# A mixer and a gated MLP on one core: the MLP's weights in three pieces instead of four, and a new order of loads and steps

## The chip, the core and the metric

The kernel runs on one core of a Trainium2 chip. The metric is the device time of one execution, in microseconds (us); the kernel before has a median of 144.99 us over three runs (144.84 to 145.03). A core has the engines TensorE (PE in the profile; its weight loads are shown apart as PEld), VectorE (DVE), ScalarE (ACT) and GpSimd (POOL), and SyncE (SP), which here only issues transfers. All work at the same time, each through its own instructions in their order.

## What is computed

`x` has 2048 tokens of D = 448 numbers, all tensors in bf16. One branch is a complex diagonal state-space model over the tokens, the other an MLP with F = 1792 hidden columns; the second gates the first.

```python
xn = layernorm(x)
# state-space branch
Lam_bar = exp(dt * Lam);  B_bar = ((Lam_bar - 1) / Lam)[:, None] * B        # Lam, B, C complex, P = 448
h[t] = Lam_bar * h[t-1] + B_bar @ xn[t]
s = 2 * real(C @ h) + xn * Dskip
# MLP branch (it normalises once more)
m = gelu(layernorm(xn) @ w1 + b1) @ w2 + b2                                   # w1 448 x 1792, w2 1792 x 448
out = x + s * silu(m)
```

## The kernel before, in words

**Tiles and stages.** The tokens are worked on in four groups of 512, each of two blocks of 256. Channels lie on the partitions: 448 rows are three tiles of 128 and one of 64, and a matmul takes 64 rows, so that two matmuls work side by side on the two halves of the rows. The hidden layer has 14 column tiles of 128, taken in seven pairs (`NF = 14`). For a group the stages are:

- statistics (L369, L373; `first_stats` L389 for group 0), the factors of the layer norm (`ln_scale`, L431 to L441) and the normalised rows for both branches, `xn` and `xn2` (L410 for the first block, L451 on VectorE and L452 on ScalarE behind it);
- the change of layout: of group 0's first block by TensorE (L415), of all else by a DMA transposition that SP issues (L77), giving `xn2T` for the MLP and `xnT` for the state-space branch;
- mm1 (L667): `xn2T` times w1, in two phases for each pair of column tiles, six matmuls and then eight; behind it gelu with b1 as its bias on ScalarE (L673). Group 0 goes block by block, with 256 columns to a matmul, since its first block is there earlier; the other groups with 512;
- mm2 (L792, L795; L853 for the last group): the hidden layer times w2, then silu on ScalarE (L798);
- bu (L698): `xnT` times the transposed B_bar (`BT`), then a copy (`ue`, `u`), the scan and the combination on VectorE (L747 to L777);
- yt (L816, L817; L866, L869 for the last group): the states times C, then the gate and the sum with x (L824; L871 and L872 for the last group) and the store.

Beside group 0, the kernel computes the constants: Lam_bar and its powers on small tiles (L491 to L584), B_bar (L600 to L602), transposed into `BT` by SP's DMA (L77, `BT<-Bn`), and combinations of C (`CZ`, `CQ`, L601 and L602) from transposed C (`Cr`, `CZ`).

**What sets the order.** Each step is recorded as a task with the names that it reads and writes. `ORDER` (L154) is one written-out list of all task numbers; each engine does its own tasks in that order, and `Plan.emit` (L99) puts a semaphore wait wherever a task needs the result of another engine or of a transfer. `SECOND` (L175) names the tasks that run on the second of two possible engines (`copy`: VectorE or ScalarE; `small`: VectorE or GpSimd). So a task that waits holds up everything behind it on its engine, and a transfer holds up the later transfers of the same issuing engine.

**The weights.** `CH` (L336) cuts the 14 column tiles into pieces of 2, 4, 4 and 4. For each piece `ldw1` (L339) makes one transfer of rows 0 to 383 and one copy that moves rows 320 to 383 to the other half of the partitions (`w1c`). The last 64 rows of w1 come in one transfer for all columns (`w1r`, L348). A column tile of a piece of n tiles is not contiguous: `fcol` (L646) takes every n-th column of the piece. w2 comes in as many transfers (L359). b1's rows are loaded as four rows on four partitions (`brows`) and turned into columns by six small matmuls in `b1_columns` (L556); Dskip's and b2's rows likewise in `skip_columns` (L563, L564).

**SP's order** before, up to the first transposition of B: x of the two first blocks (112, 112 and 224 KB), w1 piece 0 (192), w1r (224), w1 pieces 1 to 3 (384 each), the transposition of xn2 of group 0's second block, x of group 1 (448), w2 (224, 448, 448, 448), the two large pieces of B (336 each), x of group 2 (448), a small piece of B, the transposition of xn2 of group 1, the other small piece of B, x of group 3 (448), then the transpositions: xn of group 0, two of C, three of B, two of C, xn of group 1. ScalarE's queue has the three short rows of the state-space parameters, b1's rows, Dskip's and b2's.

Of the kernel before, what the change touches and what calls it, by code (L numbers as in the profile page):

```python
# [9 lines left out]
BF = dt.bfloat16  # L10
# [138 lines left out]
def dram_ap(t, offset, ap):  # L149
    return bass.AP(tensor=t.tensor, offset=offset, ap=ap)  # L150
# [1 line left out]


ORDER = [int(k) for k in """  # L154
# [19 lines left out]
""".split()]  # L174
SECOND = [int(k) for k in """  # L175
29 31 45 51 53 54 60 61 62 63 64 65 78 79 80 82 83 84 111 181 204 205 206 208 210 212 216 218 220 229 234 236 238 242 250 254 256 258 270 274 278 328
332 338 353 367 368 370 412 427 428 431 446 448 449 462 476 477 491 492 507 514 530 531 532 534 546 552 554 578 581 615 618
""".split()]


# [19 lines left out]
def bass_recurrent_scan__ssm_conv_s5__mixer_channel_mlp__prompt_kernel(  # L200
# [11 lines left out]
    L, D, F = 2048, 448, 1792  # L212
    assert tuple(A_x.shape) == (1, L, D) and tuple(B_w1.shape) == (D, F) and A_Lambda_re.shape[0] == D
    NB, NG, NF, NK = 8, 4, 14, 256
    NW, LEAD = NK + 2, 4
    NS = LEAD + NK + 2

    kb = Plan(nc)
    with ExitStack() as es:
# [3 lines left out]
        ident = SB("ident", [128, 128])  # L223
        mhalf = SB("mhalf", [128, 1, 1], F32)
        dk = SB("dk", [128, 4, NS], F32)
        iota = dk[:, 0, 0:NW]
        sgn = SB("sgn", [128, 4], F32)
        vrows = dk.bitcast(BF)[:, 1, 0:512]
        brows = vrows[32:36, :]
        cw = SB("cw", [128, 32, 4], F32)  # L230
        ang = SB("ang", [128, 5, 2, 2, 4], F32)
        eps = SB("eps", [128, 2], F32)
# [1 line left out]
        w1_sb = SB("w1_sb", [128, 4, F])  # L234
# [8 lines left out]
        drows = vrows[64:66, 64:512]  # L243
# [10 lines left out]
        gT = SB("gT", [128, 2, NF, 512])  # L254
# [25 lines left out]
        psum = es.enter_context(nc.psum_tensor("psum", [128, 8, 512], F32))  # L280
# [11 lines left out]
        def dve(fn, reads=(), writes=()):  # L292
            kb.add("dve", fn, reads, writes)
# [7 lines left out]
        def pe(fn, reads=(), writes=(), split=False):  # L301
            kb.add("pe", fn, reads, writes, split=split)
# [5 lines left out]
        with nc.Block():  # L308
# [9 lines left out]
            pool(lambda e: e.tensor_scalar(sgn[:, 1:2], sgn[:, 0:1], -TWO_PI, None, op0=ALU.mult), ["sgn"], ["sgn1"])  # L318
            pool(lambda e: e.tensor_scalar(sgn[:, 2:3], sgn[:, 0:1], TWO_PI, None, op0=ALU.mult), ["sgn"], ["sgn2"])
            pool(lambda e: e.memset(sgn[:, 3:4], math.pi / 2), ["sgn"], ["sgn3"])  # L320
            dve(lambda e: e.memset(brows[:, 256:512], 0.0), [], ["br"])
            pool(lambda e: e.memset(mhalf[:], -0.5), [], ["mhalf"])
            pool(lambda e: e.memset(eps[:, 0:1], LN_EPS), [], ["eps"])
            pool(lambda e: e.memset(eps[:, 1:2], LN_EPS * LN_EPS), ["eps"], ["eps"])
# [1 line left out]
            def ld(eng, o, i, writes, reads=()):  # L326
                kb.dma(eng, o, i, reads=reads, writes=writes)
# [4 lines left out]
            def ldx(b0, n, reads=()):  # L332
                ld("sp", x_all[:, b0:b0 + n, :, :], dram_ap(A_x, b0 * 256 * D, [[2 * D, 128], [256 * D, n], [D, 2], [1, D]]),
                   [f"x{b}" for b in range(b0, b0 + n)], reads)

            CH = ((0, 2), (2, 4), (6, 4), (10, 4))  # L336
            chunk = [c for c, (_, n) in enumerate(CH) for _ in range(n)]

            def ldw1(c):  # L339
                a, w = CH[c][0] * 128, CH[c][1] * 128  # L340
                ld("sp", w1_sb[:, 0:3, a:a + w], dram_ap(B_w1, a, [[F, 128], [128 * F, 3], [1, w]]), [f"w1_{c}"])
                copy([(w1_sb[0:64, 3, a:a + w], w1_sb[64:128, 2, a:a + w])], [f"w1_{c}"], [f"w1c_{c}"])

            for par in range(2):
                ld("sp", x_all[:, 0, par, :], dram_ap(A_x, par * D, [[2 * D, 128], [1, D]]), [f"x0p{par}"])
            ldx(1, 1)
            ldw1(0)
            ld("sp", w1_sb[64:128, 3, :], dram_ap(B_w1, 384 * F, [[F, 64], [1, F]]), ["w1r"])  # L348
            ld("act", brows[0:3, :], dram_ap(B_b1, 256, [[512, 3], [1, 512]]), ["br0"], ["br"])
            ld("act", brows[3:4, 0:256], dram_ap(B_b1, 0, [[256, 1], [1, 256]]), ["br1"], ["br"])  # L350
            for i, vec in enumerate((A_Dskip, B_b2)):
                ld("act", drows[i:i + 1, :], dram_ap(vec, 0, [[D, 1], [1, D]]), [f"dbr{i}"])
            ldw1(1)
            ldw1(2)
            ldw1(3)
            for ri, bm in enumerate((A_B_re, A_B_im)):
                ld("sp", Bn[:, ri:6:2, 0:D] if ri else Bn[:, 0:5:2, 0:D], dram_ap(bm, 0, [[D, 128], [128 * D, 3], [1, D]]), [f"Bn{ri}"])
                ld("sp", Bn[ri * 64:ri * 64 + 64, 6, 0:D], dram_ap(bm, 384 * D, [[D, 64], [1, D]]), [f"Bn6{ri}"])
            for c, (a, n) in enumerate(CH):  # L359
                ld("sp", w2_sb[:, a:a + n, :], dram_ap(B_w2, a * 128 * D, [[n * D, 128], [D, n], [1, D]]), [f"w2_{c}"])  # L360
# [193 lines left out]
                small(lambda e: e.tensor_tensor(rot[:, 0, 1, 3:4], s512[:, 3:4], sgn[:, 0:1], ALU.mult), ["as", "sgn"], ["rot01b"])  # L554

            def b1_columns():  # L556
                pe([lambda e, k=k: e.matmul(psum[:, 4, 2 + k:11 + k:4], brows[0:4, k:512:4], ident[32:36, 32:35], start=True, stop=True) for k in range(4)]
                   + [lambda e, k=k: e.matmul(psum[:, 4, k:k + 1], brows[0:4, k:256:2], ident[32:36, 35:36], start=True, stop=True) for k in range(2)],
                   ["br", "br0", "br1", "ident"], ["ps4"])
                copy([(b1f[:], psum[:, 4, 0:14])], ["ps4"], ["b1f"])  # L560

# [84 lines left out]
            def fcol(fi):  # L646
                a, n = CH[chunk[fi]]
                return slice(a * 128 + fi - a, (a + n) * 128, n)
# [200 lines left out]
            def mm2_tokens(g, q, bk):  # L849

                gb, P = g % 2, psum[:, bk, 0:D]
                copy([(P, bbc)], ["rows1"], [f"ps{bk}"])
                pe([lambda e, fi=fi: e.matmul(P, gT[:, gb, fi, 128 * q:128 * q + 128], w2_sb[:, fi, :], start=False, stop=fi == NF - 1, skip_group_check=True)  # L853
                    for fi in range(NF)], [f"gT{gb}_{fi}_{h}" for fi in range(NF) for h in range(2)] + [f"w2_{c}" for c in range(4)], [f"ps{bk}"])
                act(lambda e: e.activation(g3[:, q, :], P, ACT.Silu), [f"ps{bk}", f"Ws{g}"], [f"g3_{q}"])

            def yt_tokens(g, q, part, bk):
# [62 lines left out]
            for word in STEPS.split():  # L920
                k, g = word[0], int(word[1])
# [58 lines left out]
```

## Time and profile before

| | |
|---|---|
| median of three runs | 144.99 us (145.03, 144.99, 144.84) |
| the profiled execution | 145.18 us |
| its span, first to last instruction | 143.4 us |
| TensorE's granted clock | 1.00 |
| busy: PE, DVE, ACT, POOL | 137.7, 126.0, 105.9, 24.7 us |
| DMA: moved in all | 16.21 MB, mean 113 GB/s |

All lines of the profile come from one execution, the one of 145.18 us. Times in them count from the start of the span. A row of the timeline gives start, length, engine, line, operation, tiles and the count of instructions that it takes together; in square brackets stands the idle time of the engine before the row and what ended it. Matmuls are pipelined and their ends are modelled, so the distance of two starts says more than a length. A row of transfers gives the size and the time from issue to landing; SPq is SP's time for issuing.

### The profile page before, as it was taken

The numbers are of one execution on the slowest core, as the hardware profiler recorded it, in microseconds if no ns is written. First come the engines' busy times: TensorE is split into PE (matmuls) and PEld (weight loads), VectorE is DVE, ScalarE is ACT, GpSimd is POOL, SyncE is SP. The second block draws the span as 40 slices with busy tenths as digits, with TensorE's granted clock in tenths as the row PEclk, the third lists the DMA queues.
The fourth block names the chain that finished last, engine by engine and source line by source line (L and its number), as shares of the span: only waits on it lengthen the run. The fifth ranks groups of instructions, "written<-read, shape, count | busy, mean of one in ns | idle before, by whom it ended". The sixth has DMA issues, their size and how long they took to land.

```text
span 143.4 us, 3549 instructions
## 1 busy us (share of the span) xinstructions
PE 137.7 (96%) x1422; PEld 90.9 (63%) x1422; DVE 126.0 (88%) x275; ACT 105.9 (74%) x197; POOL 24.7 (17%) x83
## 2 busy tenths in 40 slices
PE   7999998999999989999999999999999999999991
PEld 7879953464455854566558844588777677665560
DVE  2979878998999679999999989993699998999994
ACT  3699959999996879879889359451777999928300
POOL 3389760256000700001000000200000001000000
DMA  4979997799997961010010745099830000003233
GB/s 101 240 238 249 311 331 184 152 245 184 199 189 148 151 134 35 0 32 0 7 32 0 61 108 110 0 199 193 160 126 9 0 5 0 18 5 69 49 119 128
DMA packets 38530, 16.21 MB, mean 113 GB/s; under 512 B 32937, under 2 KB 38066, under 8 KB 38514
## 3 DMA queue, kind: packets, MB, share of 16 engines
q1 hardware_dynamic: 38352, 15.92, 49.5%
q8 instruction: 11, 0.18, 0.5%
q10 hardware_dynamic: 162, 0.07, 0.2%
q14 instruction: 5, 0.04, 0.1%
HBM read 6.09 MB, written 1.84 MB: 55 GB/s over the span
## 4 chain that ended last, share of the span: by engine, by line
PE 63%; DMA 14%; DVE 13%; SPq 4%; ACT 1%; issue 1%; POOL 1%; DVEq 0%; ACTq 0%
PE psum L667 15%; PE psum L698 13%; PE psum L792 9%; PE psum L853 7%; DMA Bn<-in_A_B_re_dram 6%; PE psum L817 5%; DMA xnT<-xn_sb 5%; PE psum L816 5%; PE psum L382 3%; DMA Cr<-in_A_C_im_dram 3%; SPq L78 3%; DVE tmp L601 2%; DVE Bn L602 2%; PE psum L869 2%; PE psum L866 2%; DVE xn_sb L451 2%
## 5 line engine op out<-in xcount | busy, mean ns | idle before, releaser
L667 PE MATMUL psum<-xn2T,w_sb 64*128 64x512 bf16 (+1 forms) x490 | 46.5, 334 | 0.7 <-DMA w_sb<-in_B_w_dram 0.3
L673 ACT ACTIVATE gT<-psum,b1f 128x512 bf16<-128x512 f32 (+1 forms) x70 | 37.5, 607 | 4.5 <-PE psum L667 4.2
L667 PEld LDWEIGHTS psum<-xn2T,w_sb 64*128 64x128 bf16 x490 | 26.6, 108 | 13.9 <-ACT gT L673 1.0
L792 PE MATMUL psum<-gT,w_sb 128*128 128x512 bf16 x126 | 28.0, 379 | 0.7 <-ACT gT L673 0.6
L698 PE MATMUL psum<-xnT,BT 64*128 64x256 bf16 x392 | 25.0, 269 | 0.4 <-DVE u_sb L721 0.4
L698 PEld LDWEIGHTS psum<-xnT,BT 64*128 64x128 bf16 x392 | 19.2, 94 | 6.7 <-issue 1.0
L792 PEld LDWEIGHTS psum<-gT,w_sb 128*128 128x128 bf16 x126 | 11.9, 98 | 15.6 <-issue 1.5
L757 DVE TENSOR_TENSOR_SCAN s_w<-vs,dk 128x1048 f32<-128x1048 bf16 (+1 forms) x8 | 16.3, 2057 | 0.1
L452 ACT ACTIVATE xn_sb<-x_all,lnw 128x448 bf16<-128x448 bf16 (+2 forms) x16 | 10.0, 665 | 5.4 <-DMA xnT<-xn_sb 3.8
L853 PE MATMUL psum<-w_sb,gT 128*128 128x448 bf16 x56 | 10.9, 352 | 0.0
L474 ACT ACT_TABLE_LOAD x8 | 10.3, 1283 | 0.4
L305 ACT ACTIVATE ue<-psum 128x512 bf16<-128x512 f32 (+1 forms) x12 | 6.4, 562 | 5.3 <-PE psum L698 5.2
L451 DVE TENSOR_SCALAR xn_sb<-x_all,lnw 128x448 bf16<-128x448 bf16 (+2 forms) x24 | 8.0, 362 | 0.9 <-DVE lnw L441 0.5
L853 PEld LDWEIGHTS psum<-w_sb,gT 128*128 128x128 bf16 x56 | 5.5, 98 | 4.8 <-ACT psum L305 0.2
L305 ACT ACTIVATE vs<-s_w 64x258 bf16<-64x258 f32 (+2 forms) x11 | 6.5, 612 | 2.7 <-DVE s_w L757 2.6
L816 PE MATMUL psum<-hx,CZ 128*128 128x256 bf16 x63 | 8.4, 275 | 0.0
L817 PE MATMUL psum<-Bn,CQ 128*128 128x256 bf16 x63 | 8.2, 273 | 0.2 <-DVE Bn L777 0.2
L767 POOL TENSOR_TENSOR cur<-ang 128x8 f32<-128x8 f32 x2 | 0.4, 204 | 41.6 <-DVE ang L766 41.6
L798 ACT ACTIVATE g_sb<-psum,db 128x512 bf16<-128x512 f32 (+1 forms) x12 | 7.1, 629 | 0.6 <-PE psum L792 0.6
L369 DVE BATCH_NORM_STATS2 lnst<-x_all 128x6 f32<-128x448 bf16 x12 | 7.1, 613 | 0.4 <-DMA x_all<-in_A_x_dram 0.4
L816 PEld LDWEIGHTS psum<-hx,CZ 128*128 128x128 bf16 x63 | 5.9, 98 | 2.3 <-issue 0.4
L824 DVE TENSOR_TENSOR t<-psum,g_sb 128x512 bf16<-128x512 f32 (+1 forms) x12 | 7.1, 614 | 0.1
(161 smaller groups left out, 207.1 us busy)
## 6 DMA issues: line engine op xcount, KB each, us to landing
x_all<-in_A_x_dram SPq DMA_DIRECT2D x3, 448.0 KB, 4.3
w_sb<-in_B_w_dram SPq DMA_DIRECT2D x3, 448.0 KB, 5.3
out_dram<-Bn SPq DMA_DIRECT2D x6, 224.0 KB, 2.7
w_sb<-in_B_w_dram SPq DMA_DIRECT2D x3, 384.0 KB, 5.5
w_sb<-in_B_w_dram SPq DMA_DIRECT2D x2, 224.0 KB, 4.5
Bn<-in_A_B_im_dram SPq DMA_DIRECT2D x1, 336.0 KB, 6.5
Bn<-in_A_B_re_dram SPq DMA_DIRECT2D x1, 336.0 KB, 8.5
out_dram<-w_sb SPq DMA_DIRECT2D x3, 112.0 KB, 1.8
```

The costliest lines, as they stand in the source:

```text
L305: kb.either(("act", [lambda e, o=o, i=i: e.activation(o, i, ACT.Copy) for o, i in pairs]), ("dve", [lambda e, o=o, i=i: e.tensor_copy(o, i ...
L451: kb.either(("dve", [lambda e, o=o, i=i: e.tensor_scalar(o, i, rs, nb, op0=ALU.mult, op1=ALU.add) for o, i in parts]), ("act", [lambda e, ...
L452: ("act", [lambda e, o=o, i=i: e.activation(o, i, ACT.Identity, bias=nb, scale=rs) for o, i in parts]),
L474: kb.add("act", lambda e: e.preload_act_table_set(what), reads, writes, sem=name)
L667: return lambda e: e.matmul(dst(bk[k]), w1_sb[rows, d, fcol(2 * j + k)], rhs[rows, d], start=not second and n == 0, stop=second and n == 3)
L673: act(lambda e, k=k, fi=fi: e.activation(gT[:, gb, fi, cols], psum[:, bk[k], cols], ACT.Gelu_apprx_tanh, bias=b1f[:, fi:fi + 1]), ["b1f", ...
L698: fns.append(lambda e, rows=rows, bank=bank, m=m, o=o, n=n: e.matmul(psum[:, bank, c * NK:(c + 1) * NK].rearrange("p (b c) -> p b c", b=2) ...
L757: dve(lambda e, so=so, vi=vi, di=di: e.tensor_tensor_scan(so, vi, di, 0.0, ALU.add, ALU.mult), ["v", "vl", "vz", "dk", "dk01"] + ["v3"] * ...
L792: pe([lambda e, fi=fi: e.matmul(psum[:, bk, :], w2_sb[:, fi, 128 * j:128 * j + 128], gT[:, gb, fi, :], start=fi == 0, stop=fi == NF - 1) f ...
L816: pe([lambda e, k=k: e.matmul(par(psum[:, bk, :], 1), CZ[:, k, cols], halves(hx[:, hb, k, 1:NK + 1]), start=False, stop=k == 6, skip_group ...
L817: pe([lambda e, k=k: e.matmul(par(psum[:, bk, :], 0), CQ[:, k, cols], halves(hz[:, hb, k, :]), start=False, stop=k == 6, skip_group_check= ...
L853: pe([lambda e, fi=fi: e.matmul(P, gT[:, gb, fi, 128 * q:128 * q + 128], w2_sb[:, fi, :], start=False, stop=fi == NF - 1, skip_group_check ...
```

## The change

- `CH` has three pieces, of 4, 4 and 6 column tiles: w1 and w2 come in three transfers each (w1: 384, 384 and 576 KB; w2: 448, 448 and 672 KB) and there are three `w1c` copies. The stride in `fcol` is 4, 4 and 6 instead of 2, 4, 4 and 4.
- `w1r` is issued by ScalarE's queue, behind the three parameter rows and recorded ahead of w1's first piece.
- b1's rows are loaded by SP in two transfers (two rows of 512, one of 768) behind w1's first piece, at another place in the same scratch tile; `b1_columns` has ten small matmuls instead of six. Dskip's and b2's rows are loaded by SP behind w1's last piece.
- The new `ORDER` and `SECOND` have three tasks less (one transfer of w1, one `w1c` copy, one transfer of w2).

SP's order becomes: x of the two first blocks, w1 piece 0, b1's two transfers, w1 pieces 1 and 2, Dskip's and b2's rows, x of group 1, the transposition of xn2 of group 0's second block, the two large pieces of B, w2 (three transfers), x of group 2, a small piece of B, x of group 3, the other small piece of B, then the transpositions: xn2 of group 1, one of C, one of B, one of C, one of B, xn of group 0, the last of B, two of C, xn of group 1.

TensorE's order: mm1 of group 0 takes the pieces in nearly the same way; behind mm2 of group 0, the first bu phase of group 0 stands after 84 of the 98 mm1 matmuls of group 1 instead of after all 98, and further bu phases stand ahead of and among mm2 of group 1. At the very end, on VectorE, one product and sum of an earlier tile of tokens (L871, L872) stands behind the combination of the first half of the last scan instead of ahead of it.

Engines: on VectorE instead of GpSimd, ten small operations of a sine's polynomial (L502 to L506); on VectorE instead of ScalarE, two `w1c` copies and the copy of b1's columns; on GpSimd instead of VectorE, `ln_scale` of group 1 (five operations there, ten on VectorE), three operations that reduce an angle (L499 to L501, in the order ahead of L396 and L397 of group 0's second block) and three other small ones.

The diff, with `ORDER` and `SECOND` cut out:

```diff
@@ -152,29 +152,28 @@
 ORDER = [int(k) for k in """
...
@@ -226,7 +225,7 @@
-        brows = vrows[32:36, :]
+        brows = dk.bitcast(BF).rearrange("p i c -> p (i c)")[32:35, 2 * NS:2 * NS + 768]
@@ -318,7 +317,7 @@
-            dve(lambda e: e.memset(brows[:, 256:512], 0.0), [], ["br"])
+            dve(lambda e: e.memset(brows[:, 512:768], 0.0), [], ["br"])
@@ -333,7 +332,7 @@
-            CH = ((0, 2), (2, 4), (6, 4), (10, 4))
+            CH = ((0, 4), (4, 4), (8, 6))
@@ -344,15 +343,14 @@
             ldx(1, 1)
+            ld("act", w1_sb[64:128, 3, :], dram_ap(B_w1, 384 * F, [[F, 64], [1, F]]), ["w1r"])
             ldw1(0)
-            ld("sp", w1_sb[64:128, 3, :], dram_ap(B_w1, 384 * F, [[F, 64], [1, F]]), ["w1r"])
-            ld("act", brows[0:3, :], dram_ap(B_b1, 256, [[512, 3], [1, 512]]), ["br0"], ["br"])
-            ld("act", brows[3:4, 0:256], dram_ap(B_b1, 0, [[256, 1], [1, 256]]), ["br1"], ["br"])
-            for i, vec in enumerate((A_Dskip, B_b2)):
-                ld("act", drows[i:i + 1, :], dram_ap(vec, 0, [[D, 1], [1, D]]), [f"dbr{i}"])
+            ld("sp", brows[0:2, 0:512], dram_ap(B_b1, 0, [[512, 2], [1, 512]]), ["br0"], ["br"])
+            ld("sp", brows[2:3, :], dram_ap(B_b1, 1024, [[768, 1], [1, 768]]), ["br1"], ["br"])
             ldw1(1)
             ldw1(2)
-            ldw1(3)
+            for i, vec in enumerate((A_Dskip, B_b2)):
+                ld("sp", drows[i:i + 1, :], dram_ap(vec, 0, [[D, 1], [1, D]]), [f"dbr{i}"])
@@ -554,8 +552,8 @@
             def b1_columns():
-                pe([lambda e, k=k: e.matmul(psum[:, 4, 2 + k:11 + k:4], brows[0:4, k:512:4], ident[32:36, 32:35], start=True, stop=True) for k in range(4)]
-                   + [lambda e, k=k: e.matmul(psum[:, 4, k:k + 1], brows[0:4, k:256:2], ident[32:36, 35:36], start=True, stop=True) for k in range(2)],
+                pe([lambda e, k=k: e.matmul(psum[:, 4, k:5 + k:4], brows[:, k:512:4], ident[32:35, 32:34], start=True, stop=True) for k in range(4)]
+                   + [lambda e, k=k: e.matmul(psum[:, 4, 8 + k:9 + k], brows[:, k:768:6], ident[32:35, 34:35], start=True, stop=True) for k in range(6)],
@@ -851,7 +849,7 @@
-                    for fi in range(NF)], ... + [f"w2_{c}" for c in range(4)], [f"ps{bk}"])
+                    for fi in range(NF)], ... + [f"w2_{c}" for c in range(len(CH))], [f"ps{bk}"])
```

More of the change, by code (lines that the diff above doesn't have):

```diff
@@ L154 @@
 ORDER = [int(k) for k in """
[19 rows of a table removed]
[18 rows of a table added]
 """.split()]
 SECOND = [int(k) for k in """
-29 31 45 51 53 54 60 61 62 63 64 65 78 79 80 82 83 84 111 181 204 205 206 208 210 212 216 218 220 229 234 236 238 242 250 254 256 258 270 274 278 328
-332 338 353 367 368 370 412 427 428 431 446 448 449 462 476 477 491 492 507 514 530 531 532 534 546 552 554 578 581 615 618
+21 25 27 42 43 44 53 54 57 60 71 74 75 76 77 80 83 84 85 108 110 173 174 177 182 201 202 203 205 207 209 211 213 215 217 226 229 231 233 235 237 241
+245 249 253 270 326 331 339 360 364 399 400 429 443 446 451 459 471 472 473 487 489 515 529 542 551 561 575 578 612 615 616
 """.split()]
@@ L853, in mm2_tokens @@
                 pe([lambda e, fi=fi: e.matmul(P, gT[:, gb, fi, 128 * q:128 * q + 128], w2_sb[:, fi, :], start=False, stop=fi == NF - 1, skip_group_check=True)
-                    for fi in range(NF)], [f"gT{gb}_{fi}_{h}" for fi in range(NF) for h in range(2)] + [f"w2_{c}" for c in range(4)], [f"ps{bk}"])
+                    for fi in range(NF)], [f"gT{gb}_{fi}_{h}" for fi in range(NF) for h in range(2)] + [f"w2_{c}" for c in range(len(CH))], [f"ps{bk}"])
                 act(lambda e: e.activation(g3[:, q, :], P, ACT.Silu), [f"ps{bk}", f"Ws{g}"], [f"g3_{q}"])
```

37 rows, old and new, of the table ORDER are left out of this document.

## The prediction

> **What bounds the kernel now.** The page comes first, then the busy time by stages, then the order of TensorE's own work.
>
> ```profile
> span 143.4 us, 3549 instructions
> PE 137.7 (96%) x1422; PEld 90.9 (63%) x1422; DVE 126.0 (88%) x275; ACT 105.9 (74%) x197; POOL 24.7 (17%) x83
> ```
>
> TensorE is busy for 96% of the span, VectorE (DVE) for 88%, so the first question is where TensorE itself stands still. The windows below are the stages; their columns are the length, then PE, PEld, DVE, ACT and POOL busy, TensorE's granted clock, the DMA share and GB/s.
>
> ```profile
> 0.00:7.40 7.40, 6.23 (x68) 5.74 (x70) 4.29 (x15) 3.95 (x11) 2.98 (x20) 1.00 0.71 176
> 7.40:13.10 5.70, 5.56 (x96) 4.80 (x98) 4.88 (x22) 5.47 (x14) 4.95 (x12) 1.00 0.82 210
> 13.10:18.70 5.60, 5.60 (x105) 5.37 (x100) 5.07 (x20) 5.50 (x15) 4.53 (x19) 1.00 0.95 329
> 18.70:30.50 11.80, 11.21 (x77) 5.63 (x75) 10.41 (x41) 9.94 (x18) 3.72 (x18) 1.00 0.88 225
> 30.50:41.50 11.00, 10.80 (x102) 5.20 (x99) 10.50 (x25) 10.56 (x17) 3.35 (x5) 1.00 1.07 188
> 41.50:52.80 11.30, 10.81 (x145) 7.31 (x142) 9.68 (x24) 8.41 (x15) 2.92 (x5) 1.00 0.83 147
> 52.80:118.70 65.90, 65.73 (x702) 43.34 (x701) 59.73 (x98) 49.79 (x92) 2.00 (x6) 1.00 0.31 62
> ```
>
> From 52.8 us on TensorE is full (65.73 of 65.90), at clock 1.00: no edit there can win anything while the matmuls are the same, and the change leaves their number alone but for four tiny ones. What can be won lies ahead of 52.8 us: the first 7.4 us, in which the real matmuls have not begun, and 0.59 + 0.20 + 0.49 = 1.28 us of idle time in the three windows from 18.7 to 52.8. Where those are, TensorE's timeline shows (start, length, work, count, idle before and releaser):
>
> ```profile
> 21.80 0.81 PE L792 MATMUL psum<-gT,w_sb 128*128 128x512 bf16 x3
> 23.20 5.77 PE L792 MATMUL psum<-gT,w_sb 128*128 128x512 bf16 x26 [0.59 <-ACT gT L673]
> ...
> 30.55 3.84 PE L667 MATMUL psum<-xn2T,w_sb 64*128 64x512 bf16 x34
> 34.60 7.14 PE L667 MATMUL psum<-xn2T,w_sb 64*128 64x512 bf16 x64 [0.20 <-ACT gT L673]
> 41.57 0.82 PE L698 MATMUL psum<-xnT,BT 64*128 64x256 bf16 x12
> 42.52 3.19 PE L792 MATMUL psum<-gT,w_sb 128*128 128x512 bf16 x14
> 45.65 2.58 PE L698 MATMUL psum<-xnT,BT 64*128 64x256 bf16 x44
> ...
> 49.81 0.83 PE L698 MATMUL psum<-xnT,BT 64*128 64x256 bf16 x12
> 51.00 1.26 PE L698 MATMUL psum<-xnT,BT 64*128 64x256 bf16 x20 [0.36 <-DVE u_sb L721]
> ```
>
> A matmul's end is modelled late, so I count from start to start, with a steady pitch from an undisturbed row. mm2: 5.77/26 = 0.22, so three end at 21.80 + 0.66 = 22.46 and the hole to 23.20 is 0.74. mm1 of 512 columns: (41.57 - 34.60)/64 = 0.109, so 34 end at 34.25 and the hole to 34.60 is 0.35. bu: 2.58/44 = 0.059, so 12 take 0.70; the holes at 42.52 and 51.00 are 0.25 and 0.49. Together 1.83 us: what the changed order could win here at most.
>
> **The change part by part.** First the start, up to the first real matmul (L667).
>
> ```profile
> 2.18 2.73 SPq L78 DMA_DIRECT2D w_sb<-in_B_w_dram  x5
> w_sb<-in_B_w_dram SPq DMA_DIRECT2D x1, 224.0 KB, 4.6
> 6.11 0.57 ACT L305 ACTIVATE xn2T<-psum 128x512 bf16<-128x512 bf16 x1
> 6.11 0.30 PE L557 MATMUL psum<-ident,dk 4*128 4x3 bf16 x4
> 7.36 11.41 PE L667 MATMUL psum<-xn2T,w_sb 64*128 64x256 bf16 x196 [0.34 <-DMA w_sb<-in_B_w_dram]
> ```
>
> SP issues five w1 transfers in 2.73 us, 0.55 each; the 224 KB of w1's last rows are the second, so they start at about 2.7 and land 4.6 later, at 7.3. That is what the first L667 matmul waits for; its other operand is ready at 6.11 + 0.57 = 6.68. With these rows on ScalarE's queue, ahead of the first w1 piece, they no longer stand last. In their place the first piece grows from 192 to 384 KB and two loads of b1's rows follow it on SP. Lower bound: the first matmul at 6.68, a gain of 0.68. Upper bound: x (448 KB), the rows (224) and the piece (384) make 1056 KB where 864 had to land; the 192 KB more take 0.58 at the 329 GB/s of the window from 13.1. In addition there are ten little b1 matmuls instead of six, which were hidden behind the wait; four more at 0.30/4 are 0.30 if nothing hides them, so +0.88. By 7.40 the chip had moved 176 x 7.4 = 1302 KB, more than the 1056 KB, so the new order of bytes need not be late. I take +0.1, between ends of -0.68 and +0.88.
>
> The w1 pieces 2 and 3 now have one transfer and one 64-row copy (L305/L306) less behind them. The copies go from ScalarE to DVE; DVE is idle for 5.70 - 4.88 = 0.8 us and 5.60 - 5.07 = 0.5 us in the two windows from 7.4 to 18.7, which covers them. Dskip's and b2's rows move from ScalarE's queue to SP behind w1: 0.55 each of SP's time; behind them stands x of group 1, which gains more than that (below). Zero.
>
> ```profile
> 9.48 1.33 SPq L77 DMA_TRANSPOSE xn2T<-xn_sb  x1
> xn2T<-xn_sb SPq DMA_TRANSPOSE x1, 3.2
> 9.70 0.19 POOL L431 TENSOR_SCALAR lnw<-lnmv 128x4 f32<-128x4 f32 x1
> 12.95 0.48 POOL L435 TENSOR_SCALAR lnw<-lnw 128x8 f32<-128x8 f32 x1
> ```
>
> The second block of group 0 lands at 9.48 + 3.2 = 12.68 and TensorE comes to it at 7.36 + 98 x 11.41/196 = 13.07: 0.4 of slack. In the new order GpSimd does three more little operations of about 0.2 ahead of that block's square root, so the transposition lands about 0.6 later, and TensorE waits **+0.2** (0 to +0.5).
>
> Now x of group 1 and B ahead of w2.
>
> ```profile
> 15.21 1.68 DVE L369 BATCH_NORM_STATS2 lnst<-x_all 128x6 f32<-128x448 bf16 x3 [0.39 <-DMA x_all<-in_A_x_dram]
> 21.24 1.09 ACT L452 ACTIVATE xn_sb<-x_all,lnw 128x384 bf16<-128x384 bf16 x2 [1.52 <-DVE xn_sb L451]
> ```
>
> The hole of 0.74 at 22.46 is a queue on ScalarE: the two gelus that mm2 needs stand behind group 1's normalisation, which takes ScalarE from 21.24 to 22.33 and waited 1.52 for its turn because x of group 1 landed only at 15.2. In the new order x stands right behind w1: with the first 448 KB of x and w1's 1568, its own 448 end 2464 KB, of which 1302 have moved by 7.4; the other 1162 at 210 to 329 GB/s make 10.9 to 12.9, say 12. This hole goes. What takes its place could be w2: x (896 KB, two groups), w1 with its rows (1568), B (672) and w2 (1568) are 4704 KB. The windows moved 1302 + 1197 + 1842 = 4341 KB by 18.7, then 225 KB per us; with some 230 KB of transposition w2's end is at 18.7 + 593/225 = 21.3. Its last piece is wanted about where the hole stands now, at 22.5, so 1.2 us to spare; if it came later than that, mm2 would wait for the difference. On the other side, group 1's scale (L431 to L435) moves from DVE to GpSimd, where group 0's took 9.70 to 13.43 = 3.7 us. If all of that came on top, the 3.2 that x gains would cover most of it, and DVE's own steps for it are gone. The holes of 0.35 at 34.60 (gelu's table late), 0.25 and 0.49 go because group 1's work is done earlier and the bu phases are spread among mm1: **-1.83** for all four (-0.74 if it is the first alone).
>
> The price of the new order is on SP's queue of transpositions:
>
> ```profile
> 22.45 2.91 SPq L77 DMA_TRANSPOSE xn2T<-xn_sb  x1
> ...
> 26.72 3.25 SPq L77 DMA_TRANSPOSE xnT<-xn_sb  x1
> ...
> 33.70 9.83 SPq L77 DMA_TRANSPOSE BT<-Bn  x3
> BT<-Bn SPq DMA_TRANSPOSE x3, 5.0
> ```
>
> Now group 0's xnT goes out at 26.72, right behind group 1's xn2T. In the new order two transpositions of C and two of B go between them. The two of C took the time from 26.72 + 3.25 = 29.97 to 33.70, 3.73 together; one of B takes 9.83/3 = 3.28. If xn2T goes out at 22.0, a little before the 22.45 of now, xnT is issued at 22.0 + 2.91 + 3.73 + 6.56 = 35.2 at the latest and lands 5.0 later (the row of B's; its own kind follows it in the queue as those do), at 40.2; I take 39.9, as B's first one then finds its operand long ready. TensorE wants xnT earlier than before: the first bu phase now stands after 84 of the 98 mm1 matmuls. With mm1 of group 1 begun at about 30.0 (30.55 - 0.74 + 0.2), that is 30.0 + 84 x 0.109 = 39.1. So TensorE waits **+0.8**; ends 0 and +2.4 (xn2T at 23.3). DVE's writes of group 1's xn buffer wait for the same transposition, and have the mm2 of group 1 as cover.
>
> ```profile
> 139.81 1.06 DVE L871 TENSOR_TENSOR w_sb<-psum,w_sb 128x448 bf16<-128x448 f32 x2 [0.16 <-PE psum L866]
> ```
>
> At the end, DVE takes one product and sum of an earlier token tile after the last scan's half instead of before it. One L871 is 0.53 and DVE has only 0.16 idle there: **+0.3** (0 to +0.5).
>
> Sum: +0.1 + 0.2 - 1.83 + 0.8 + 0.3 = **-0.43**. The span becomes 143.4 - 0.4 = 143.0; the profiled execution, 145.18, is 1.78 more than its span, so 144.75 there. The median of the runs, 144.99, is 0.19 under the profiled execution: 144.56, say 144.5.
>
> **The rivals.** *xnT too late* (slower). SP's queue is serial and DMA's share is already 1.07 from 30.5 to 41.5. The gain is used up when xnT lands at 39.9 + 0.5 = 40.4 rather than 39.9; at 41.5, which an xn2T sent out at 23.3 gives (36.5 + 5.0), the wait is 2.4 instead of 0.8: 144.5 + 1.6 = 146.1; the middle of this case, between 145.3 and 146.1 and with a tail above, is 145.9. For it: DVE is busy 10.41 of 11.80 from 18.7 on, and B's scaling, which two of the transpositions need, is its work. Against it: x and B are there about 3 us earlier, so that scaling can begin earlier.
>
> *The start pays for the bytes.* If all 16 DMA engines are shared, the rows on ScalarE's queue bring nothing and the first matmul pays +0.88 instead of +0.1: 145.3, no measurable change or barely slower. For it: shares of 0.71 and 0.82 around 7.4 us. Against: the 1302 KB. [...]
>
> *Weights at a stride of six.* A piece of six tiles holds a tile's columns six elements apart. The nearest rows are the weight loads at a stride of two and of four:
>
> ```profile
> L667 PEld LDWEIGHTS psum<-xn2T,w_sb 64*128 64x128 bf16 x10 | 0.6, 97 | 0.0
> L667 PEld LDWEIGHTS psum<-xn2T,w_sb 64*128 64x128 bf16 x6 | 0.3, 110 | 0.0
> ```
>
> 97 ns and 110 ns; carried on, some 125 ns at six. The two row halves of a pair run side by side, each with its own load. With 256 columns a matmul takes 0.053 us (5.60/105, the gapless window) to 0.058 (11.41/196), so a pair takes 107 to 116 ns and the 42 pairs of six tiles in two blocks could each lose 9 to 18 ns: 0.4 to 0.75 us; nothing with 512 columns, where a pair takes 218 ns. That makes up to 145.2: no change. Against: 110 is over 107 already, and the window has no idle time. [...]
>
> *Hidden anyway.* The holes are only moved: mm2 waits for w2 or the table instead of the gelus. Then -0.74 or so is not won: 145.2.
>
> **How the numbers follow.** The forecast 0.5, with its own range 143.8 to 145.0. xnT too late 0.22. The start 0.12. Stride six 0.08. Hidden anyway 0.08. About 0.2%, 0.29 us, is what a measurement of this kernel tells from no change: 144.70 to 145.28. The forecast gives 0.44 faster and 0.06 same; the three small rivals together (0.28) 0.08 faster, 0.15 same, 0.05 slower; xnT 0.02 same, 0.20 slower: 0.52, 0.23, 0.25. The range, 143.3 to 146.0: below, xnT just in time (-0.8) and the start at a gain; above, the middle of the xnT case.
>
> **What would show it.** Right: the first L667 matmul at 7.1 to 7.8, the second block at 13.2 to 13.5, no mm2 wait for a gelu at 22 us, mm1 of group 1 at 29.7 to 30.2, one wait of 0.3 to 1.5 for xnT at 39 us and no other hole over 0.3 until 52. Wrong: a first matmul at 8 or later; a pair pitch over 120 ns in tiles 8 to 13; a wait for w_sb in mm2; a bu that starts after 41; or new idle time of TensorE behind 52 us, which I count at nothing.

## The result, and the profile after

The changed kernel takes 145.99 us (median of five runs, 145.68 to 146.59) against 144.84 for the kernel before in the same session: 0.84% slower, ratio 1.0084 with a 95% interval of 1.0057 to 1.011. A second session gave 1.0105 (1.0054 to 1.0156). The forecast was 144.5, faster. All lines of the profile after come from one execution, of 146.59 us.

```profile
span 144.9 us, 3550 instructions
PE 136.8 (94%) x1422; PEld 92.1 (64%) x1426; DVE 126.3 (87%) x280; ACT 102.8 (71%) x190; POOL 26.9 (19%) x79
```

The span is some 1.4 us longer (144.86 against 143.45 before rounding). Where, three coarse windows of each kernel tell (columns as in the prediction); first before, then after.

```profile
5.00:55.00 50.00, 48.25 (x548) 31.09 (x546) 44.28 (x136) 43.85 (x85) 21.04 (x63) 1.00 0.91 206
55.00:97.00 42.00, 41.83 (x395) 26.49 (x395) 40.38 (x68) 31.44 (x56) 1.58 (x4) 1.00 0.26 48
97.00:140.00 43.00, 43.00 (x445) 29.15 (x442) 37.91 (x63) 28.40 (x52) 0.67 (x3) 1.00 0.26 62
```

```profile
5.00:55.00 50.00, 47.28 (x568) 33.02 (x569) 45.54 (x143) 40.49 (x76) 21.78 (x57) 1.00 0.87 206
55.00:97.00 42.00, 41.84 (x372) 26.21 (x373) 38.81 (x66) 33.57 (x59) 2.08 (x5) 1.00 0.32 55
97.00:140.00 43.00, 43.00 (x447) 28.58 (x442) 38.53 (x63) 26.64 (x50) 1.35 (x3) 1.00 0.18 47
```

TensorE's idle time from 5 to 55 us was to fall; by these windows it rose from 1.75 to 2.72 us. About 0.5 of that rise is not real: for 126 weight loads of mm2 the trace has only 122 matmuls, and three of the four missing records each leave a stretch of 0.16 us marked "issue" before 55 us.

```profile
L790 PE MATMUL psum<-gT,w_sb 128*128 128x512 bf16 x122 | 27.0, 379 | 0.6 <-issue 0.6
L790 PEld LDWEIGHTS psum<-gT,w_sb 128*128 128x128 bf16 x126 | 12.0, 98 | 14.5 <-issue 0.4
```

So the idle time is some 2.2 us, still not less than before. From 55 to 140 the two are alike, and TensorE's last matmuls end at 140.44 and 140.54. So the 1.4 us lie behind TensorE's end. TensorE's timeline of the changed kernel shows what became of the holes:

```profile
7.50 6.05 PE L665 MATMUL psum<-xn2T,w_sb 64*128 64x256 bf16 x98
14.85 5.54 PE L665 MATMUL psum<-xn2T,w_sb 64*128 64x256 bf16 x98 [1.30 <-ACT gT L671]
...
20.82 9.01 PE L790 MATMUL psum<-gT,w_sb 128*128 128x512 bf16 x41 [0.16 <-issue]
29.77 1.72 PE L793 MATMUL psum<-gT,w_sb 128*64 128x256 bf16 x28
31.42 9.30 PE L665 MATMUL psum<-xn2T,w_sb 64*128 64x512 bf16 x84
40.94 0.83 PE L696 MATMUL psum<-xnT,BT 64*128 64x256 bf16 x12 [0.23 <-DMA xnT<-xn_sb]
```

mm2 of group 0 (20.82) runs without a hole where 0.74 us stood, and mm1 of group 1 (31.42) without the one of 0.35. But the second block begins only at 14.85, 1.3 us after the first block's end. The releaser named there, a gelu, is not it: the block's transposition, issued at 9.78, landed 4.9 us later, at 14.7.

```profile
xn2T<-xn_sb SPq DMA_TRANSPOSE x1, 4.9
```

The end, on SP's queue (start, length of issuing), before and after:

```profile
135.35 2.17 SPq L78 DMA_DIRECT2D out_dram<-Bn  x2
139.74 1.79 SPq L78 DMA_DIRECT2D out_dram<-w_sb  x4
```

```profile
138.80 0.81 SPq L78 DMA_DIRECT2D out_dram<-Bn  x2
141.48 1.79 SPq L78 DMA_DIRECT2D out_dram<-w_sb  x4
```

VectorE's steps that count here, before and after (the sums into `Bn` are group 2's, those into `w_sb` the last group's):

```profile
133.61 0.22 DVE L841 TENSOR_TENSOR Bn<-Cr,x_all 128x128 bf16<-128x128 bf16 x1
134.78 0.55 DVE L838 TENSOR_TENSOR Bn<-Cr,x_all 128x768 bf16<-128x768 bf16 x1
...
139.08 0.56 DVE L872 TENSOR_TENSOR w_sb<-w_sb,x_all 128x448 bf16<-128x448 bf16 x2
...
140.79 0.57 DVE L872 TENSOR_TENSOR w_sb<-w_sb,x_all 128x448 bf16<-128x448 bf16 x2
```

```profile
137.25 0.55 DVE L836 TENSOR_TENSOR Bn<-Cr,x_all 128x768 bf16<-128x768 bf16 x1
137.72 0.38 DVE L870 TENSOR_TENSOR w_sb<-w_sb,x_all 128x448 bf16<-128x448 bf16 x1
...
138.56 0.21 DVE L839 TENSOR_TENSOR Bn<-Cr,x_all 128x128 bf16<-128x128 bf16 x1
...
140.89 0.45 DVE L870 TENSOR_TENSOR w_sb<-w_sb,x_all 128x224 bf16<-128x224 bf16 x2
```

VectorE ends at 141.34, where it ended at 141.36 before. Yet the first of SP's four last stores, whose data was there at 137.72 + 0.38 = 138.10, goes out at 141.48, 3.4 us later, and from there all four follow in a row. From VectorE's end to the end of the span it is 3.5 us; before, 2.1. SP is done with issuing group 2's stores at 139.61 and then stands for 1.9 us, and no engine's work ends that wait.

It stands in the function that writes out the program, `Plan.emit`: at the fourth of SP's tasks from the end, SP waits for all transfers recorded so far.

```python
settle = [t for t in order if t.eng == "sp"][-4]
...
if t is settle:
    for sem, val in self.counts.items():
        if val and sem not in ENGS and seen.get(sem, 0) < val:
            eng.wait_ge(self.sems[sem], val)
```

In both kernels those transfers include group 2's two stores (`out_dram<-Bn`). The new order computes two of their sums (L836, L839; L838 and L841 before) between the last group's, so the stores go out at 138.80 to 139.6 instead of 135.35 to 137.5, and take 2.1 us to land. Only then may the last group's stores start.

The section on the change says that a product and a sum of L871 and L872 moved behind the first half of the last scan's combination. That is wrong: in `ORDER` these steps stand behind both halves in either kernel. What moved are the two sums of group 2, from ahead of that combination to behind the first product of the last group, and with them group 2's two stores.

### The profile page after: what moved, and what is told of

It is laid out like the page before. It is cut to its first block, busy times and chain, and to the rows that moved or that the text cites. A ratio compares the mean times of both kernels' runs of the same rounds, so it can differ in the third digit from the quotient of the medians.

```text
span 144.9 us, 3550 instructions
## 1 busy us (share of the span) xinstructions
PE 136.8 (94%) x1422; PEld 92.1 (64%) x1426; DVE 126.3 (87%) x280; ACT 102.8 (71%) x190; POOL 26.9 (19%) x79
## 4 chain that ended last, share of the span: by engine, by line
PE 67%; DVE 6%; DMA 3%; ACT 2%; issue 1%; SPq 0%; DVEq 0%
PE psum L665 16%; PE psum L696 15%; PE psum L790 12%; PE psum L851 7%; PE psum L814 5%; PE psum L815 5%; DMA xnT<-xn_sb 3%; DVE Bn L600 2%; PE psum L793 2%; PE psum L864 2%; PE psum L819 2%; ACT WT L582 2%; DVE tmp L599 2%; DVE w_sb L869 1%; PE psum L867 1%
## 5 line engine op out<-in xcount | busy, mean ns | idle before, releaser
L665 PEld LDWEIGHTS psum<-xn2T,w_sb 64*128 64x128 bf16 x490 | 27.4, 116 | 14.0 <-ACT gT L671 2.2
L790 PE MATMUL psum<-gT,w_sb 128*128 128x512 bf16 x122 | 27.0, 379 | 0.6 <-issue 0.6
L765 POOL TENSOR_TENSOR cur<-ang 128x8 f32<-128x8 f32 x3 | 2.3, 757 | 55.3 <-DVE ang L764 55.3
L472 ACT ACT_TABLE_LOAD x8 | 10.3, 1283 | 0.4
L449 DVE TENSOR_SCALAR xn_sb<-x_all,lnw 128x448 bf16<-128x448 bf16 (+2 forms) x29 | 9.5, 358 | 0.3 <-DMA xnT<-xn_sb 0.2
L304 ACT ACTIVATE vs<-s_w 64x258 bf16<-64x258 f32 (+2 forms) x14 | 7.9, 571 | 2.4 <-DVE s_w L755 2.3
L814 PE MATMUL psum<-hx,CZ 128*128 128x256 bf16 x63 | 7.9, 275 | 0.0
L431 POOL TENSOR_TENSOR lnw<-lnw,mhalf 128x8 f32<-128x8 f32 x4 | 7.2, 1812 | 0.3
```

Of the source, the lines that this page charges most:

```text
L304: kb.either(("act", [lambda e, o=o, i=i: e.activation(o, i, ACT.Copy) for o, i in pairs]), ("dve", [lambda e, o=o, i=i: e.tensor_copy(o, i ...
L449: kb.either(("dve", [lambda e, o=o, i=i: e.tensor_scalar(o, i, rs, nb, op0=ALU.mult, op1=ALU.add) for o, i in parts]), ("act", [lambda e, ...
L472: kb.add("act", lambda e: e.preload_act_table_set(what), reads, writes, sem=name)
L665: return lambda e: e.matmul(dst(bk[k]), w1_sb[rows, d, fcol(2 * j + k)], rhs[rows, d], start=not second and n == 0, stop=second and n == 3)
L790: pe([lambda e, fi=fi: e.matmul(psum[:, bk, :], w2_sb[:, fi, 128 * j:128 * j + 128], gT[:, gb, fi, :], start=fi == 0, stop=fi == NF - 1) f ...
L814: pe([lambda e, k=k: e.matmul(par(psum[:, bk, :], 1), CZ[:, k, cols], halves(hx[:, hb, k, 1:NK + 1]), start=False, stop=k == 6, skip_group ...
```

## The experiments

The theory of the end: SP's collective wait, now behind later stores, costs 1.4 us. Its rival: VectorE's order alone, as the prediction had it. In the edits `move(a, b)` puts task a ahead of task b in `ORDER`; what stands behind a # is added here.

**e1_tail**, the end put back:

```diff
+move(638, 654)  # q01
+move(636, 655)  # o01
+move(640, 662)  # store of block 1
+move(639, 671)  # store of block 0
```

> The changed kernel with group 2's last two sums on VectorE and the two stores of group 2 put back to where they stood before (ahead of the last scan's combination). Theory: the 1.4 us lost behind TensorE's end is SP waiting, ahead of its four last stores, for group 2's stores to land; so the span falls by 1.3 to 1.5 us against the changed kernel and the last four stores go out from about 139.8 instead of 141.5. Rival: only VectorE's own order costs, the 0.3 us of the prediction; then it falls by 0.3 or less, and the stores still go out at about 141.

Measured: 145.12 us, ratio to before 1.001 (0.9984 to 1.0035); span 143.6.

```profile
135.89 1.34 SPq L78 DMA_DIRECT2D out_dram<-Bn  x2
138.94 3.06 SPq L78 DMA_DIRECT2D out_dram<-w_sb  x4
```

**e2_settle**, no task moved:

```diff
-        settle = [t for t in order if t.eng == "sp"][-4]
+        settle = [t for t in order if t.eng == "sp"][-6]
```

> The changed kernel with nothing moved, but SP's collective wait for all earlier transfers put ahead of its sixth store from the end instead of the fourth, so that it no longer covers group 2's stores. Theory of SP's wait: the span falls by 1.2 to 1.4 us although VectorE's order is the changed one. Rival (VectorE's order, or the last stores colliding on the DMA engines): no change, within 0.3 us.

Measured: 145.12 us, ratio 1.0015 (0.9991 to 1.0039); span 143.8.

```profile
139.10 0.81 SPq L78 DMA_DIRECT2D out_dram<-Bn  x2
139.96 2.19 SPq L78 DMA_DIRECT2D out_dram<-w_sb  x4
```

Group 2's stores are as late as in the changed kernel, but the last ones no longer wait for them. The span fell by 1.1 us with VectorE's order untouched, which the rival excludes. The stretch from VectorE's end to the end of the span says it without what happens earlier in an execution: it is 2.24 us in e1, e2 and all the later kernels that are built on e1, 2.1 in the kernel before, p1 and p2, and 3.5 to 3.8 in the four profiles of kernels whose wait covers late stores (after, after_again, e3, e4).

**e3_before_late**, the kernel before with the late sums and stores:

```diff
+move(639, 685)  # o01
+move(641, 685)  # q01
+move(643, 694)
+move(642, 694)
```

> The kernel before with only this done: group 2's last two sums on VectorE and its stores behind the product of the first token tile, as in the changed kernel. Theory of SP's wait: 1.0 to 1.5 us slower than before. Rival (VectorE's order alone): 0.3 us slower or less.

Measured: 146.83 us, ratio 1.0132 (1.0087 to 1.0176): 1.9 us slower, more than expected. From VectorE's end to the end of the span it is 3.8 us, 1.7 more than before; that is SP's wait. But VectorE itself also ends later here, at 142.20 instead of 141.36: the two moved sums (0.55 and 0.22) stand among the last group's. So the edit costs by both theories, and it is e2, not this run, that separates them. Without the wait (e1, e2) the change is level with before: everything else of it nets to nothing.

Why nothing? First suspect: the second block's late transposition.

**e4_w2_first**: `move(34, 32)`, w2's first piece behind it instead of B's.

> The changed kernel with the first piece of w2 (rows of 3584 B) instead of the first piece of B (rows of 896 B) right behind the transposition of group 0's second block on SP's queue. Theory a: the small packets of B hold up the last completions of the transposition; then its landing goes from 4.9 to about 3.3 us, the hole of 1.3 us at 14.85 closes and the span falls by up to 1.3 us. Rival b: an instruction fetch of 16 KB, which runs for 0.94 us on one of the DMA engines just when the transposition ends, holds them up, and the follower doesn't matter; then the hole stays at 1 us or more.

Measured: 147.08 us, ratio 1.0135 (1.0098 to 1.0173). The transposition landed after 3.8 us and the hole before the second block shrank to 0.18, but the first bu phase then waited 2.05 us for xnT and began at 41.67. Closing the hole won nothing, since the next bound lies behind it; the run without an edit says the same. Whether the order of the loads made the landing late, this run can't tell, because the late landing also goes away without an edit.

**after_again**, nothing edited.

> The changed kernel once more, nothing edited. If the late landing of the second block's transposition comes from an instruction fetch that falls at another time in each execution, then the fetch ahead of 14 us and the hole before the second block differ from the first profile (12.68 us, 1.3 us); if it comes from the order of the loads, both are the same again.

Measured: 146.30 us, ratio 1.0105; the fetch at 10.15 us, landing after 3.1 us, no hole before the second block, mm1 of group 1 at 30.52 instead of 31.42, and yet:

```profile
30.52 9.29 PE L665 MATMUL psum<-xn2T,w_sb 64*128 64x512 bf16 x84
40.85 0.83 PE L696 MATMUL psum<-xnT,BT 64*128 64x256 bf16 x12 [1.03 <-DMA xnT<-xn_sb]
```

The first bu phase begins at 40.85, as at 40.94 in the first profile. xnT's landing sets it.

**before_again**, nothing edited.

> The kernel before once more, nothing edited. Same question: with the fetch as the cause, its time differs from the 12.07 us of the first profile, and if it falls between 10.5 and 12 us the second block's transposition lands late here too; with the order of loads as the cause it lands at about 12.7 us again.

Measured: one run, 144.19 us; the second block's transposition landed after 3.2 us, as in the first profile of that kernel, so this run doesn't tell the two causes apart. Its profile shows something else too: of the four holes that the prediction counted, those of 0.35 (in mm1 of group 1) and of 0.49 (between the bu phases) are not there, with nothing edited.

```profile
30.64 10.89 PE L667 MATMUL psum<-xn2T,w_sb 64*128 64x512 bf16 x98
...
49.60 2.49 PE L698 MATMUL psum<-xnT,BT 64*128 64x256 bf16 x42
```

**e5_xnt_early**: e1_tail with `move(184, 219)`, xnT ahead of B's transpositions.

> The changed kernel with its end put right as in e1_tail, and group 0's transposition xnT ahead of the first transposition of B on SP's queue, so that only one of C stands ahead of it. Theory: after mm1 the next bound is xnT's landing (40.9 to 41.7 us in the runs so far); it should now land by 36, the wait for it (0.2 to 2.0 us) goes, and the first bu phase begins at 39.7, or at 40.7 if the second block is late; the time falls by 0.5 to 1.0 us against e1_tail, to 144.1 to 144.6. Rival: the transpositions of B, each now 1.1 us later, become the bound instead, and nothing is won (145.1).

Measured: 145.91 us, ratio 1.0082 (1.005 to 1.0113). The rival held in its mechanism: the same phase begins at 40.82 and waits for B instead. But the time is 0.8 us above the rival's 145.1; a second wait of 0.6 us, for ScalarE, is new, and the rest was not traced.

```profile
PE psum L706 <- DMA BT<-Bn: 1.4, 1, 1.4
PE psum L706 <- ACT tmp L608: 0.6, 1, 0.6
```

**e6_xn_before_wt**: e1_tail with `move(182, 197)`, the one ScalarE step for which VectorE stood still.

> The changed kernel with its end put right as in e1_tail, and one ScalarE step moved: the last normalisation of group 0 (27.1 us in the changed profile), for which VectorE stands still for 1.03 us, ahead of the four conversions of the state tables at 24.71. Theory: the first bu phase waits for a chain that runs through VectorE's scaling of B and SP's serial transpositions, and this is its one slack; so that phase begins at 39.8 to 40.2 instead of 40.8 to 41.3 and the time falls by 0.5 to 1.0 us against e1_tail. Rival: SP's queue alone, from the moment when xn2T goes out (24.0), sets it; then the first bu phase stays at 40.8 or later and nothing is won.

Measured: 145.03 us, ratio 1.0008 (0.9976 to 1.0039). The rival held: the phase begins at 40.80. SP's queue shows why; each transposition occupies SP for 1.5 to 3.1 us, and each row starts where the one before ends:

```profile
24.26 2.16 SPq L77 DMA_TRANSPOSE xn2T<-xn_sb  x1
26.47 1.55 SPq L77 DMA_TRANSPOSE Cr<-in_A_C_re_dram  x1
28.07 3.14 SPq L77 DMA_TRANSPOSE BT<-Bn  x1
31.24 1.97 SPq L77 DMA_TRANSPOSE Cr<-in_A_C_im_dram  x1
33.26 2.85 SPq L77 DMA_TRANSPOSE BT<-Bn  x1
36.15 1.92 SPq L77 DMA_TRANSPOSE xnT<-xn_sb  x1
```

**e8_xn2_early**: e6 with `move(268, 206)`, `move(269, 206)`, `move(270, 206)`, `move(271, 206)` and task 270 on VectorE.

> The kernel of e6_xn_before_wt with group 1's xn2 written earlier: VectorE writes all of it (also the part that ScalarE wrote behind its gelus) right behind its factors, ahead of two steps of the state tables and of B's scaling. Theory: SP issues transpositions without a pause from the moment when group 1's xn2T goes out (24.26 to 36.15 us in e6_xn_before_wt), so that moment, and not mm1, sets the first bu phase; xn2T now goes out at 22.3 to 22.8, xnT lands by 39.5, its wait of 1.0 us falls to 0.3 or less, and the time falls by 0.5 to 1.0 us against e6_xn_before_wt, to 144.1 to 144.5. Rival: B's scaling on VectorE, now later, becomes the bound for the transposition of B behind it, so that xnT still lands at 40.5 or later and nothing is won.

Measured: 145.39 us, ratio 1.0047 (1.0021 to 1.0074), if anything slower than e6. Again the rival:

```profile
23.04 2.90 SPq L77 DMA_TRANSPOSE xn2T<-xn_sb  x1
25.98 1.33 SPq L77 DMA_TRANSPOSE Cr<-in_A_C_re_dram  x1
28.66 1.93 SPq L77 DMA_TRANSPOSE BT<-Bn  x1
```

xn2T goes out 1.2 us earlier, but SP then stands from 27.31 to 28.66 for B's scaling, which VectorE, busy with xn2 before, ends only then. xnT goes out at 35.91 and the phase begins at 40.57. VectorE's work and SP's queue are about equally long up to that point; none of the three moves (e5, e6, e8) wins anything.

**p1_x_first**: the kernel before with `move(40, 144)`, x of group 1 ahead of the transposition.

> The kernel before with one move: x of group 1 is loaded ahead of the transposition of group 0's second block instead of behind it. Theory of the prediction: the hole of 0.74 us at 22.46, where mm2 waits for two gelus behind a late normalisation, goes and the time falls by 0.5 to 0.74 us. Rival: hidden anyway, because B's transpositions set when the first bu phase of group 0 can run; then the hole goes but the time stays within 0.3 us.

Measured: 144.29 us, ratio 0.9964 (0.9939 to 0.9989): 0.5 us faster than before; this kernel and p2, which contains its move, are the only ones here that beat the kernel before.

```profile
22.66 5.77 PE L798 MATMUL psum<-gT,w_sb 128*128 128x512 bf16 x26 [0.18 <-ACT gT L679]
```

The hole before this row is down from 0.59 to 0.18, and the first bu phase, which in this kernel stands behind all of mm1, waits for nothing.

**p2_x_first_settle**: p1 with the edit of e2.

> The kernel before with x of group 1 loaded ahead of the second block's transposition (p1_x_first), and SP's collective wait put ahead of its sixth store from the end. If that wait costs something in the kernel before too (its four last stores go out together at 139.4 to 141.2, where the first has its data at about 138.9), the time falls by another 0.2 to 0.4 us below 144.29. Rival: the last store is ScalarE's, which goes out behind VectorE's last sum in any case; then nothing changes.

Measured: 144.34 us, ratio 0.9962 (0.9929 to 0.9996), the same as p1. The expectation had the wrong store in mind: in the kernel before the first of the four needs the third of the last group's sums (L872, 139.08 + 0.56 = 139.64), and goes out at 139.74. Where group 2's stores are early, the collective wait is free.

**e7_w1r_on_sp**, e1_tail with w1's last rows on SP's queue again:

```diff
-            ld("act", w1_sb[64:128, 3, :], ...
+            ld("sp", w1_sb[64:128, 3, :], ...
+move(19, 22)
```

> The changed kernel with its end put right as in e1_tail, and w1's last rows issued by SP again, behind the first piece of w1. Theory: another queue brings no bandwidth, since the transfers share the DMA engines, and the first real matmul (7.4 to 7.9 us in the changed runs) moves by 0.3 us at most; the time stays within 0.3 us of e1_tail, as xnT sets the first bu phase anyway. Rival: the start is worth its difference; then the first matmul is at 8.2 or later and the time rises by 0.5 us.

Measured: 145.04 us, ratio 0.9999 (0.9969 to 1.0029); the first mm1 matmul starts at 7.69, against 7.46 in e1_tail and 7.44 to 8.03 in all profiles that have these rows on ScalarE's queue. Which queue these rows take is worth nothing that can be measured.

## Why the prediction was wrong

**The step that failed** is the last term: "One L871 is 0.53 and DVE has only 0.16 idle there: +0.3". The end cost 1.4 us (3.5 against 2.1 from VectorE's end to the span's end), and e1 and e2 took 1.1 to 1.3 us of span back. The term priced a step that doesn't move (L871 stands behind both halves of the combination in either kernel) and looked at VectorE alone. What moved were group 2's last two sums, with group 2's stores behind them, and SP's wait for those stores stands ahead of the last four. VectorE itself ended where it did before, so what the term priced was not what cost. The wait is in the code of before, but its profile couldn't show it: there the stores go out 0.1 us behind the sum that the first of them needs. None of the signs that the prediction named looks behind TensorE's end.

**The gain of 1.83** failed too: with the end put right the kernel is level with before (145.12 us, e1 and e2), where the other four terms came to -0.73. The profiles show two reasons. First, the 1.83 was read from one execution. In before_again 0.84 of it (0.35 and 0.49) is not there. The holes at 22.46 and 34.60 are closed in the changed kernel, and p1 shows 0.5 us for the first alone (0.16 to 0.88 by its interval). Second, the first bu phase was brought forward to a point where its operands weren't there. I had xnT landing at 39.9 and TensorE there at 39.1. It landed at 40.8, since xn2T went out at 24.0 and not at 22.0 (SP's queue after):

```profile
24.00 1.98 SPq L77 DMA_TRANSPOSE xn2T<-xn_sb  x1
...
36.32 1.92 SPq L77 DMA_TRANSPOSE xnT<-xn_sb  x1
xnT<-xn_sb SPq DMA_TRANSPOSE x1, 4.5
```

The last row is xnT's time from issue to landing. x of group 1 did come earlier, but the steps that write xn2 stand behind other work on VectorE and ScalarE. The wait, forecast at +0.8, was 0.2 us in this profile, where the second block is late as well, and 0.67 (e7) to 2.05 (e4) where it is not; 1.03 in after_again. In after_again, whose trace has all matmuls, the idle time from 5 to 55 us is 1.90, where 1.75 stood before. That the early bu phase uses up the gain is argued from these waits: no run put it back behind all 98 matmuls of mm1.

**The rival "xnT too late"** names this wait, and its 145.9 us is next to the 145.99 measured. That is luck: without SP's wait at the end, of which it says nothing, the kernel takes 145.12.

**Second block, +0.2**: 1.3 us in the first profile, nothing in after_again. The transposition was issued 0.3 and 0.7 us later than before, where I had 0.6; a landing 4.9 us after issue, as in the first profile, I had not foreseen.

**The start, +0.1**: 7.50 against 7.36 in the first two profiles. But it differs by more than that from execution to execution: 7.24 to 8.12 in the five profiles with the loads of before, 7.44 to 8.03 in the eight with the changed ones, with means of 7.57 and 7.64. So +0.1 can't be told from nothing. What TensorE waits for there is not w1 now but b1's rows, whose ten matmuls stand ahead of mm1:

```profile
7.02 0.27 PE L555 MATMUL psum<-ident,dk 3*128 3x2 bf16 x4 [0.44 <-DMA dk<-in_B_b_dram]
```

The rival's 0.88 did not come. What it says of queues did. In the first profile of the changed kernel the packets of ScalarE's queue (q10) take 94.6% of 16 engines' time from 4.0 to 4.5 us, in which most of w1's last rows move, and those of SP's queue (q1) 12.2%; from 4.5 to 5.0 us it is 10.8% and 95.5%. Where one queue moves much, the other moves little, and the sum stays at 106 to 107%. w1's first piece and its last rows land there at 6.8 and 5.7 us, and b1's rows let TensorE go on at 7.02; in e7 they do so at 7.20, which is 0.2 later and less than two executions differ. By e7 another queue for w1's last rows brings nothing that can be measured.

**Stride six**: the row of the loads for the six-tile piece (11.7 to 13.1 us):

```profile
L665 PEld LDWEIGHTS psum<-xn2T,w_sb 64*128 64x128 bf16 x28 | 1.6, 121 | 0.0
```

121 ns against the 125 that I extrapolated, but TensorE was busy throughout that window (1.40 of 1.40 us), and no hole followed. The load does get dearer, and evenly: 97, 110 and 121 ns at strides of 2, 4 and 6.

**w2 in time, hidden work**: no wait for w_sb in mm2, right.

## What to carry to other kernels

Make sure which step a new order moves, and follow it through every queue that it feeds, to its last transfer and to whoever waits for that; a collective wait near the end turns any late store into delay for all that stand behind it (here 1.4 us). A hole in the busiest engine is worth its length only if the next operand is early by as much: before you bring a consumer forward, sum up the serial queue that makes its operand, from the moment when that queue can really start. Read the holes in two executions before you add them up: two of four were there in one only. When the parts of a new order are tried alone, one may win (here x of group 1 first, 0.5 us) while the whole loses.

## What the runs showed of the hardware

The second block's transposition landed after 3.1 to 3.8 us in nine of the profiles of this study and after 4.5 to 5.0 us in five (the first of the changed kernel, e1, e3, e8 and p2). In the first profile of the changed kernel 30 packets of 4 bytes start between 12.23 and 12.48 us and the next two at 13.60 and 13.62; the landing came at 14.7. The first profile of the kernel before has 32 such packets between 11.93 and 12.16, and the landing at 12.68. In the window from 12.5 to 12.8 us the changed kernel has one packet of the instruction queue:

```profile
q8 instruction: 1, 0.02, 19.6%
```

It is 16 KB long, starts at 12.68 and takes 0.94 us, which fills most of the pause between the 30 packets and the two. In the kernel before such a packet starts at 12.07, and in after_again, the same program as the changed kernel, at 10.15; there the landing came after 3.2 and 3.1 us. In e2, e5 and e6 one starts by 10.3, with landings after 3.1, 3.1 and 3.2 us. In the other eight profiles none starts between 9.5 and 10.2 us, and four of them landed late and four did not. No run moved the fetch alone: that it held up the landing in the first profile of the changed kernel, where the wait of 1.3 us stands beside it, is my guess and not shown.
